# A planner that runs twice and holds each load back until a fixed time ahead of its first use

## The chip, the cores and the metric

The kernel runs on one core of a Trainium2 chip. The metric is the device time of one execution in microseconds (us); lower is better. The kernel before took 425.89 us as the median of three runs (425.65 to 426.75).

## The reference

Two stages follow each other on `B = 4` batches of `N = 12800` rows of width `C = 128`. First an attention through 49 agents: `softmax(agents k^T) v` gives 49 rows per batch (`agent_v`), and `softmax(q agents^T) agent_v` gives one row per query. Then a gated convolution: a causal depth-wise convolution of 5 taps over the rows, a sigmoid of it as the gate, `x @ w_val` as the value, and the product of both through `w_out`:

```
a2k     = sm(agents, k);  agent_v = a2k @ v
x       = sm(q, agents) @ agent_v
gate    = sigmoid(sum_k conv_w[k] * x[t-4+k])
out     = (gate * (x @ w_val)) @ w_out
```

## The kernel before

**Units and chunks.** A batch is cut into 10 units of 1280 rows. Three inputs are loaded unit by unit: `k` and `q` (640 KB each, transposed on the host) and `v` (645 KB). That makes 120 loads. The output is made in 100 chunks of 512 columns, 25 per batch.

**What a unit costs.** TensorE (PE) makes scores of a `k` unit or a `q` unit (L376, 16 matmuls), and for `v` the agent sums (L480). For a `q` unit VectorE, GpSimd (POOL) and ScalarE make the softmax weights `pt`; a DMA transpose (`x<-pt`, L835) turns them into the tile `x1`, and two more DMAs (`x<-x`, L884, "shifts" below) copy shifted rows of `x1` into the tile `x2`. For the first four units PE makes the transposition instead. After the second unit of a pair POOL copies a halo of 4 columns (L819, or a memset, L816) into the next segment of `x1`.

**What a chunk costs.** PE makes the gate (five matmuls on `x1`, L922, and one on `x2`, L926), the value (L949, L953) and the projection of the chunk two before (L992 to L994); ScalarE the tanh (L935), VectorE the product `h` (L962), ScalarE and POOL its two halves `hh` and `hl` (L968, L973), ScalarE the output tile (L1006), and a DMA stores two chunks together (L1021).

**Batches overlap.** While the chunks of one batch run, `k`, `v` and `q` of the next are worked on. In the last batch only its own `q` is left to load. When the last `v` of a batch is through, a short series of small steps (`fold_weights`) makes the weights for its chunks.

**Slots.** The loads share a ring of `NLOAD = 11` tiles (`ld`). Load number n may start when PE has read load n - 11 for the last time. Every load, transpose, shift and store (but one small load at the start) is issued from one queue, that of SyncE (SP), in one order; an issue that waits holds up all that is behind it.

**The planner.** The program does not emit instructions at once. Each piece of work is added to a `Plan` as a step: its engine, an estimated duration, what it reads and writes, and, for a DMA, how long it occupies the wires. `Plan.order()` then plays the steps through, with a clock of its own, one at a time: each engine takes the ready step whose chain of work behind it (`tail`) is longest; a DMA may start when the wires are at most `BACKLOG = 3.0` us behind (L129) and the eighth DMA before it has landed (`LANES = 8`). PE is an exception: each PE step is chained to the one before (L101 to L104), so the order of work on PE is the written order in the string `order` (L1088), whatever the clock says. `order()` returns the steps sorted by their planned start, and the program issues them in that order (L1141). On the chip only this order remains: no engine waits for a planned time.

A load has no input, so in the planner it becomes ready the moment its slot is free (`at = [0.0] * n`, L117, later raised to the end of the slot's last reader).

Of the kernel before, what the change touches and what calls it, by code (L numbers as in the profile page):

```python
# [58 lines left out]
BACKLOG = 3.0  # L59
LANES = 8  # L60
LAND = 1.4

QS = 256.0
WS = 64.0
# [3 lines left out]
class Plan:  # L68
# [11 lines left out]
    def add(self, engine, us, fn, reads=(), writes=(), moved=0.0, key=None, urge=0.0):  # L80
        i = len(self.steps)
        need = set()
        for x in reads:
            need |= self.wrote.get(x, set())
        for x in writes:
            need |= self.wrote.get(x, set()) | self.read.get(x, set())
        for x in reads:
            self.read.setdefault(x, set()).add(i)
        for x in writes:
            self.wrote[x], self.read[x] = {i}, set()  # L90
        self.steps.append((engine, us, fn, need, moved, key))
        self.urge.append(urge)

    def order(self):
        n = len(self.steps)
        after = [[] for _ in range(n)]
        last = None
        for i, (engine, us, fn, need, moved, key) in enumerate(self.steps):
            for j in need:
                after[j].append(i)  # L100
            if engine == "pe":  # L101
                if last is not None and last not in need:
                    after[last].append(i)
                last = i  # L104
        tail = [0.0] * n
        for i in reversed(range(n)):
            engine, us, fn, need, moved, key = self.steps[i]
            cost = us + HOP + (moved + LAND if moved else 0.0)
            if engine == "pe":
                cost = us  # L110
            tail[i] = cost + self.urge[i] + max((tail[j] for j in after[i]), default=0.0)
        engines = ("pe", "act", "dve", "pool", "dma")
        free = dict.fromkeys(engines, 0.0)
        wire = 0.0
        lanes = [0.0] * LANES
        left = [len(s[3]) for s in self.steps]
        at = [0.0] * n  # L117
        queues = {e: [] for e in engines}
        pe = [i for i, s in enumerate(self.steps) if s[0] == "pe"]
        here = 0  # L120
        for i, s in enumerate(self.steps):
            if s[0] != "pe" and not left[i]:
                queues[s[0]].append(i)
        start = [0.0] * n
        kind = None
        done = 0
        while done < n:
            best = None
            free["dma"] = max(free["dma"], wire - BACKLOG, lanes[0])  # L129
            for e in engines:  # L130
                if e == "pe":
                    if here < len(pe) and not left[pe[here]]:
                        pick, when = pe[here], max(free[e], at[pe[here]])
                    else:
                        continue
                elif queues[e]:
                    q = queues[e]
                    soon = min(max(free[e], at[i]) for i in q)
                    open_ = [i for i in q if at[i] <= soon + 0.05]
                    pick = max(open_, key=lambda i: (tail[i], -i))  # L140
                    for i in q:
                        if tail[i] > tail[pick] + 1.0 and at[i] < soon + 0.6 * self.steps[pick][1]:
                            pick = i
                    when = max(free[e], at[pick])
                else:
                    continue
                if best is None or when < best[0]:
                    best = when, e, pick
            when, e, i = best
            engine, us, fn, need, moved, key = self.steps[i]  # L150
            if e == "pe":
                here += 1
                if key != kind:
                    when += 0.12
                kind = key
            else:
                queues[e].remove(i)
            start[i] = when
            free[e] = when + us
            end = when + us + HOP  # L160
            if moved:
                wire = max(wire, when + 0.5) + moved
                end = max(wire, when + us) + LAND
                lanes = lanes[1:] + [end]
            done += 1
            for j in after[i]:
                if i in self.steps[j][3]:
                    left[j] -= 1
                    at[j] = max(at[j], end)
                    if not left[j] and self.steps[j][0] != "pe":  # L170
                        queues[self.steps[j][0]].append(j)
        self.start = start
        return sorted(range(n), key=lambda i: (start[i], i))


@with_exitstack
def tile_agent_attention_gated_conv(
# [22 lines left out]
    plan = Plan()  # L200
    add = plan.add

    def ring(n, shape, dtype, name, pool=const):
        return [pool.tile(shape, dtype, name=f"{name}{i}") for i in range(n)]

    ld = ring(NLOAD, [P, VW], F32, "ld")
# [147 lines left out]
    def load(kind, b, u):  # L354
        i = taken[0] % NLOAD
        taken[0] += 1
        slot_of[kind, b, u] = i
        if kind == "v":
            dst, src = ld[i], vP[b, u].rearrange("p n c -> p (n c)")
        else:  # L360
            dst = ld[i][:, 0:UNIT]
            src = (kT if kind == "k" else qT)[b, :, u * UNIT : (u + 1) * UNIT]
        parts = [(dst, src, [("ld", i), ("ld2", i)])]
        if (kind, b, u) == ("v", 0, NU - 1):
            h = VW // 2
            parts = [(dst[:, 0:h], src[:, 0:h], [("ld", i)]), (dst[:, h:], src[:, h:], [("ld2", i)])]
        for d, f, keys in parts:
            add(
                "dma", 0.4, lambda d=d, f=f: nc.sync.dma_start(out=d, in_=f), (), keys,
                1.57 / len(parts),  # L370
            )

    def score_matmuls(b, src, out):
# [662 lines left out]
    at = (0, 2, 5, 7, 10, 12, 15, 17, 20, 22)  # L1036
# [94 lines left out]
    for w in work:  # L1131
        if w[0] in "qkv":
            while ahead < min(len(loads), NLOAD + done):
                load(*loads[ahead])
                ahead += 1
                if ahead == W_AT:
                    weights()
            done += 1
        run[w[0]](*w[1:])

    for i in plan.order():  # L1141
        plan.steps[i][2]()


# [42 lines left out]
```

## Time and profile before

| | |
|---|---|
| median of three runs | 425.89 us |
| profiled execution, span from first to last instruction | 423.6 us |
| PE busy | 403.9 us (95%) |
| VectorE, ScalarE, POOL busy | 293.3, 301.5, 228.2 us |
| mean granted TensorE clock | 0.985 |
| moved by DMA | 127.62 MB, mean 301 GB/s |

The profile page gives the span of the profiled execution and no other time of it; the median is 2.3 us above the span, which is what lies before the first and after the last instruction. A granted clock of 1.00 is TensorE's upper level of 2.4 GHz, 0.50 is the lower one of 1.2 GHz. "DMA share" is the mean over the 16 DMA engines of the time in which packets were under way; packets of one engine overlap, so it can pass 1. In the tables SPq is SyncE's queue: a start there is the issue of a DMA, and its duration is how long the issue held the queue, not the transfer.

### The profile page before, as it was taken

The numbers are of one execution on the slowest core, as the hardware profiler recorded it, in microseconds if no ns is written. First come the engines' busy times: TensorE is split into PE (matmuls) and PEld (weight loads), VectorE is DVE, ScalarE is ACT, GpSimd is POOL, SyncE is SP. The second block draws the span as 40 slices with busy tenths as digits, with TensorE's granted clock in tenths as the row PEclk, the third lists the DMA queues.
The fourth block names the chain that finished last, engine by engine and source line by source line (L and its number), as shares of the span: only waits on it lengthen the run. The fifth ranks groups of instructions, "written<-read, shape, count | busy, mean of one in ns | idle before, by whom it ended". The sixth has DMA issues, their size and how long they took to land.

```text
span 423.6 us, 10042 instructions
## 1 busy us (share of the span) xinstructions
PE 403.9 (95%) x3907; PEld 197.0 (47%) x3907; DVE 293.3 (69%) x562; ACT 301.5 (71%) x521; POOL 228.2 (54%) x263
## 2 busy tenths in 40 slices
PE   4979999999999999999999899999999989999995
PEld 1358434346555443446555343335555534344443
DVE  3757899867875978667795575767765678676231
ACT  1564568779966777678876486778876567788776
POOL 1002557654657565554566355574366277877553
PEclk9969999999999999999999899999999999999998
DMA  8999999999999999999999999999999977755733
GB/s 320 420 417 411 370 367 353 301 295 310 412 293 283 346 317 362 304 278 356 351 379 324 271 299 370 314 332 302 296 393 322 239 196 161 199 163 176 205 121 124
DMA packets 75129, 127.62 MB, mean 301 GB/s; under 512 B 50466, under 2 KB 50850, under 8 KB 75084
## 3 DMA queue, kind: packets, MB, share of 16 engines
q1 hardware_dynamic: 74940, 126.87, 96.9%
q8 instruction: 30, 0.49, 0.5%
q10 hardware_dynamic: 144, 0.13, 0.2%
q14 instruction: 15, 0.12, 0.1%
HBM read 79.25 MB, written 26.21 MB: 249 GB/s over the span
## 4 chain that ended last, share of the span: by engine, by line
PE 78%; DMA 9%; DVE 8%; ACT 1%; POOL 1%; issue 1%; SPq 0%; POOLq 0%; DVEq 0%; ACTq 0%
PE gate L922 23%; PE sc L376 17%; PE av L480 10%; PE val L949 5%; PE out L992 5%; PE val L953 5%; PE gate L926 5%; PE out L993 4%; DMA ld<-kT 4%; PE out L994 4%; DMA x<-pt 3%; DMA x<-x 2%; DVE h L962 1%; DVE qw L772 1%; DVE qsm L763 1%
## 5 line engine op out<-in xcount | busy, mean ns | idle before, releaser
L973 POOL TENSOR_TENSOR hl<-h,hh 128x512 f16<-128x512 f32 (+1 forms) x101 | 116.9, 1158 | 96.1 <-ACT hh L968 96.0
L922 PE MATMUL gate<-x,stat 128*128 128x512 f16 (+1 forms) x500 | 125.2, 380 | 0.2 <-ACT th L935 0.2
L962 DVE SCALAR_TENSOR_TENSOR h<-th,val 128x512 f32<-128x512 f32 x100 | 67.8, 678 | 66.8 <-PE out L993 26.2
L376 PE MATMUL sc<-ld,ag_sb 128*32 128x320 f32 x1280 | 101.5, 447 | 7.6 <-DMA ld<-kT 7.0
L935 ACT ACTIVATE th<-gate,unscale 128x512 f32<-128x512 f32 x100 | 68.3, 683 | 33.3 <-PE gate L926 31.7
L1006 ACT ACTIVATE ob<-out,oscale 128x512 f32<-128x512 f32 x98 | 67.3, 687 | 21.3 <-PE out L994 20.1
L922 PEld LDWEIGHTS <-stat 128*128 128x128 f16 x505 | 46.3, 97 | 63.7 <-issue 14.8
L968 ACT CAST hh<-h 128x512 f16<-128x512 f32 (+1 forms) x101 | 61.5, 609 | 17.2 <-DVE h L962 16.4
L750 POOL TENSOR_TENSOR qw<-sT,qmx 128x490 f32<-128x490 f32 x40 | 41.4, 1035 | 47.6 <-DVE qmx L745 47.5
L376 PEld LDWEIGHTS sc<-ld,ag_sb 128*32 128x32 f32 x1280 | 36.7, 111 | 59.4 <-issue 25.7
L480 PE MATMUL av<-ld,eT 128*32 128x129 f32 (+1 forms) x1400 | 50.7, 279 | 1.0 <-DVE eT L386 1.0
L480 PEld LDWEIGHTS av<-ld,eT 128*32 128x32 f32 (+1 forms) x1400 | 47.1, 117 | 7.5 <-issue 2.5
L794 POOL TENSOR_TENSOR pt<-qw,pt 128x490 f16<-128x490 f32 x40 | 44.8, 1120 | 3.1 <-ACT pt L779 2.9
L471 ACT ACTIVATE e<-ks,kbias 128x320 f32<-128x320 f32 x80 | 39.3, 554 | 5.4 <-DVE eT L386 3.3
L386 DVE STREAM_TRANSPOSE sT<-sc 128x640 f32<-128x640 f32 x40 | 33.6, 839 | 13.4 <-PE sc L376 12.7
L402 ACT COPY ks<-sc 128x640 f32<-128x640 f32 x40 | 27.7, 691 | 21.2 <-PE sc L376 19.1
L386 DVE STREAM_TRANSPOSE eT<-e 128x640 f32<-128x640 f32 x40 | 33.5, 842 | 9.8 <-ACT e L471 5.2
L926 PE MATMUL gate<-x,stat 95*128 95x512 f16 x100 | 38.3, 383 | 1.5 <-DMA x<-x 1.5
L949 PE MATMUL val<-x,stat 128*128 128x512 f16 x100 | 38.2, 382 | 0.8 <-DVE h L962 0.6
L953 PE MATMUL val<-x,stat 95*128 95x512 f16 x100 | 38.1, 381 | 0.0
L994 PE MATMUL out<-hl,wo 128*128 128x512 f16 x98 | 37.0, 378 | 1.1 <-POOL hl L973 1.1
L992 PE MATMUL out<-hh,wo 128*128 128x512 f16 x98 | 37.3, 381 | 0.1
(130 smaller groups left out, 389.4 us busy)
## 6 DMA issues: line engine op xcount, KB each, us to landing
ld<-kT SPq DMA_DIRECT2D x40, 640.0 KB
ld<-qT SPq DMA_DIRECT2D x40, 640.0 KB
ld<-vP SPq DMA_DIRECT2D x39, 645.0 KB
outT<-ob SPq DMA_DIRECT2D x48, 512.0 KB
x<-x SPq DMA_DIRECT2D x18, 375.0 KB
x<-x SPq DMA_DIRECT2D x18, 100.0 KB
outT<-ob SPq DMA_DIRECT2D x3, 256.0 KB
x<-x SPq DMA_DIRECT2D x4, 187.5 KB
```

Of the source, the lines that this page charges most:

```text
L376: nc.tensor.matmul(out=out[g * BLK : (g + 1) * BLK, j, 0:GT], lhsT=ag_sb[:, b, j * BLK : (j + 1) * BLK], rhs=src[:, g * GT : (g + 1) * GT] ...
L386: nc.vector.transpose(out=out.rearrange("p n (j i) -> p j n i", j=2), in_=in_.rearrange("p j (n i) -> p j n i", i=BLK),)
L480: nc.tensor.matmul(out=av[o + j : o + j + cols, 0 : C + 1], lhsT=et[:, n, j : j + cols], rhs=vt[:, n, :], start=(u == 0 and n < 2), stop=( ...
L922: nc.tensor.matmul(out=pg, lhsT=stat[:, k, :], rhs=x1[:, c : c + w], start=(k == 0), stop=False,)
L926: nc.tensor.matmul(out=pg, lhsT=stat[0 : TAPS * X2R, TAPS + 1, :], rhs=x2[0 : TAPS * X2R, o2 : o2 + w], start=False, stop=True,)
L935: lambda: nc.scalar.activation(out=th, in_=pg, func=AF.Tanh, scale=unscale[:, 0:1]),
L949: nc.tensor.matmul(out=pv, lhsT=stat[:, TAPS, :], rhs=x1s[(b * NCH + n0 // CH) // 5 % NX][:, PAD + o2 : PAD + o2 + w], start=True, stop=False,
L953: nc.tensor.matmul(out=pv, lhsT=stat[0 : TAPS * X2R, TAPS + 2, :], rhs=x2[0 : TAPS * X2R, o2 : o2 + w], start=False, stop=True,)
L962: lambda: nc.vector.scalar_tensor_tensor(out=h, in0=th, scalar=1.0, in1=pv, op0=ALU.add, op1=ALU.mult),
L968: "act", 0.16 + 0.42 * scale, lambda: nc.scalar.copy(out=hh, in_=h),
L973: lambda: nc.gpsimd.tensor_tensor(out=hl, in0=h, in1=hh, op=ALU.subtract),
L1006: lambda: nc.scalar.activation(out=ob[:, o : o + w], in_=po, func=AF.Copy, scale=oscale),
```

## The change

A constant `AHEAD = 14.0` is added; loads get the key `"ld"`; `order()` takes a list of earliest times; and a new method runs `order()` once, reads from it when each load's first reader starts, and runs it again with each load held back to 14 us before that. Nothing else differs. It all happens while the program is built.

```
-    def order(self):
+    def order(self, held=None):
...
-        at = [0.0] * n
+        at = list(held or [0.0] * n)
...
+    def late_loads(self):
+        self.order()
+        held = [0.0] * len(self.steps)
+        for i, s in enumerate(self.steps):
+            for j in s[3]:
+                if self.steps[j][5] == "ld":
+                    t = self.start[i] - AHEAD
+                    held[j] = min(held[j], t) if held[j] else t
+        return self.order(held)
...
             add(
                 "dma", 0.4, lambda d=d, f=f: nc.sync.dma_start(out=d, in_=f), (), keys,
-                1.57 / len(parts),
+                1.57 / len(parts), key="ld",
             )
...
-    for i in plan.order():
+    for i in plan.late_loads():
         plan.steps[i][2]()
```

## Rows read from the trace of the kernel before

**Rows 1.** The page: busy time of the engines, then DMA share in 40 slices.
```profile
PE 403.9 (95%) x3907; PEld 197.0 (47%) x3907; DVE 293.3 (69%) x562; ACT 301.5 (71%) x521; POOL 228.2 (54%) x263
...
DMA  8999999999999999999999999999999977755733
```

**Rows 2.** Stretches of 10 us: busy time of each engine, PE clock, DMA share, GB/s.
```profile
core 0: us, PE busy (x) PEld busy (x) DVE busy (x) ACT busy (x) POOL busy (x), PEclk, DMA share, GB/s
10.00:20.00 10.00, 9.32 (x120) 3.72 (x111) 7.54 (x15) 4.88 (x8) 0.00 (x0) 1.00 1.02 419
...
230.00:240.00 10.00, 8.50 (x107) 4.72 (x100) 5.10 (x14) 3.67 (x7) 4.97 (x7) 0.85 1.14 290
240.00:250.00 10.00, 10.00 (x84) 4.63 (x83) 7.23 (x21) 7.23 (x14) 5.70 (x8) 0.98 1.11 270
...
370.00:380.00 10.00, 10.00 (x50) 4.35 (x52) 7.11 (x13) 8.82 (x16) 8.52 (x10) 1.00 0.64 176
```

**Rows 3.** Waits of PE over the span: us in total, times, longest.
```profile
PE sc L376 <- DMA ld<-kT: 7.0, 4, 6.1
PE gate L926 <- DMA x<-x: 1.5, 1, 1.5
...
PE out L994 <- POOL hl L973: 1.1, 1, 1.1
```

**Rows 4.** Chain that ended last: start us, us, what; near 10, 230 and 335 us.
```profile
7.55 12.53 DMA ld<-kT
...
220.73 7.50 DMA x<-pt
...
228.28 7.34 DMA x<-x
...
331.87 6.86 DMA x<-pt
...
338.78 0.19 POOL x L819
```

**Rows 5.** Timeline of SP's queue: start us, us the queue was held, what.
```profile
10.73 16.74 SPq L369 DMA_DIRECT2D ld<-vP  x11
...
212.77 7.23 SPq L835 DMA_TRANSPOSE x<-pt  x1
...
228.28 1.65 SPq L884 DMA_DIRECT2D x<-x  x2
...
266.97 1.73 SPq L369 DMA_DIRECT2D ld<-vP  x2
...
326.31 2.14 SPq L369 DMA_DIRECT2D ld<-qT  x2
...
361.24 2.94 SPq L835 DMA_TRANSPOSE x<-pt  x2
...
366.46 1.65 SPq L884 DMA_DIRECT2D x<-x  x2
```

**Rows 6.** Chain that ended last, where PE first uses loads.
```profile
26.12 14.19 PE av L480 x200
...
294.50 2.34 PE av L480 x80
...
368.32 1.21 PE sc L376 x16
...
379.83 1.21 PE sc L376 x16
```

**Rows 7.** Timeline of PE: three uses of loads around 220 us.
```profile
219.25 2.41 PE L480 MATMUL av<-ld,eT 128*32 128x129 f32 x80
...
228.85 1.28 PE L376 MATMUL sc<-ld,ag_sb 128*32 128x320 f32 x16
...
241.20 2.09 PE L376 MATMUL sc<-ld,ag_sb 128*32 128x320 f32 x28
```

**Rows 8.** Waits of SP's queue over the span: us in total, times, longest.
```profile
SPq L835 <- POOL hl L973: 48.4, 17, 8.1
```

More of the change, by code (lines that the diff above doesn't have):

```diff
@@ L61 @@
 LAND = 1.4
+AHEAD = 14.0
 QS = 256.0
```

## The prediction

> **What bounds the kernel now.** I read the page first, then the waits of PE, then the chain around the few gaps of PE, then the queue from which the DMAs are issued. PE is busy 403.9 of 423.6 us [rows 1], and the order of its work is written out by hand and not touched, so the change can only move PE's 19.7 idle us and the stretches of low clock. Most of that idle time is out of reach: at the start PE waits 7.0 us for the first keys [rows 3], which no hold can bring sooner, and the rest of the start and the end are short dependent chains. In the body two gaps remain, and both end with a DMA. (A) At 234 us PE waits 1.5 us for a shift, the only wait of that kind [rows 3]. Its chain is a transpose issued at 220.73 that took 7.50 us and a shift issued at 228.28 that took 7.34 us [rows 4]. After the gap the granted clock is 0.85 in that stretch and 0.98 in the next [rows 2]: TensorE falls from 2.4 to 1.2 GHz for a while, which costs 1.5 + 0.2 = 1.7 us more. (B) At 339 us PE waits 1.1 us for `hl` [rows 3], because POOL, in order, sits before the halo copy until a transpose issued at 331.87 lands 6.86 us later, and only then can make `hl` [rows 4].
>
> The second resource is the DMA: its share is above 1 from 10 to 340 us and 0.64 at 370 to 380 [rows 2]. The reader should see the same transposes in both regimes: from the issue of the transpose to the issue of the shift that waits for it is 228.28 - 220.73 = 7.6 us in the crowded part [rows 4, 5], and 366.46 - 361.24 = 5.2 us for a pair of them, so 3.7 us for the second (it starts some 1.5 us later), in the empty part [rows 5]. One transpose even holds SP's queue for 7.23 us at 212.77, where a pair held it for 2.94 us at 361.24 [rows 5].
>
> **What the loads do now.** At the start a load is issued 15.4 us before its use (v: 10.73 against 26.12), later much sooner: 294.50 - 266.97 = 27.5 us, and the last query tile 379.83 - 327.4 = about 52 us [rows 5, 6]. Between, a load can go out as soon as PE frees a slot, 11 loads ahead of its use. So the crowd in the DMA engines is in part work that is not due for 25 us.
>
> **The change, part by part.** It adds and removes no instruction of the chip: the first planner run, the list of holds and the key cost 0 us, since they run at build time. What it moves are the issues of about 85 of the 120 loads (all but the first 35 or so, whose lead is already near 14 us or limited by DMA rate), each later by its present lead less 14: some 10 us in the body, up to 38 us for the last one. A load is moved on SP's queue behind the transposes, shifts and stores that the plan starts in between. On the chip there is no wait for a time: SP issues the load when it gets there.
>
> *Effect on (A).* With a hold the loads issued in 205 to 230 us would be those used 14 us later. PE uses loads at 219.25 (two), then nothing until 228.85 and 229.95, then 241.20 [rows 7]. So loads would go out near 205 to 206.5, three near 215 to 217, and the next at 227. Before the transpose at 212.77, there would be none for 6 us, where now one is ahead whenever a slot came free. Three loads of 0.66 MB at 419 GB/s [rows 2] are 1.57 us each, 4.7 us, over by about 221, and the second transpose at 220.7 and its shift meet an almost empty queue until 227. I take the 7.6 us from transpose to shift down to the quiet 3.7 to 5.2, a gain of 2.4 to 3.9 us, and the shift's 7.34 down by 1 to 2 us. PE needs only 1.5 of that. What is late next is the ordinary chain of a chunk (tanh, product, halves), which PE does not wait for in the chunks around. Bounds: 0 (if the softmax weights of VectorE, not the DMA, set the transpose's time) to -(1.5 + 1.7) = -3.2 us. I take -3.2, because the whole surplus is more than the gap.
>
> *Effect on (B).* The loads before the transpose are now two query tiles at 326.31 that PE uses at 368.32 and 379.83 [rows 5, 6]; they would go at 354.3 and 365.8. I count that an earlier tile, now long there, comes in instead of one of them, so the queue is shorter by one load, 1.57 us, and the transposes ahead stay. Bounds 0 to -1.1 us, taken -0.6.
>
> *What it costs.* Loads that were 15 us early now have a margin of 14 us less the time from issue to landing. The crowded start shows that at its longest: a key tile issued at 7.55 landed 12.53 us later [rows 4]. Held alone, a load still lands 1.5 us before its use. But behind a blocked transpose (7.23 us [rows 5]) it would land 12.53 + 7.23 - 14 = 5.8 us late, and PE would lose that and the 1.7 us of clock that followed gap (A). Bounds 0 to +7.5 us. I take +0.6: near zero, because the long landing time and the long block belong to the crowd that the hold thins out.
>
> Sum: -3.2 - 0.6 + 0.6 = -3.2 us against the profiled span of 423.6. The 2.3 us that lie around the span stay, so from the median: 425.9 - 3.2 = 422.7 us.
>
> A rule speaks against the change. The Trainium skill, "DMA: Bandwidth & Descriptors", section "Rules for kernel authors", tells authors to issue a DMA early, compute, and wait for it late, so that its fixed cost is hidden. This trace agrees only in that no load after the start makes PE wait; by the rule the later issue can only lose, and the time would be that of rival 1 below. What it leaves out, and rows 4 and 5 show, is that an early load delays the urgent transfers queued behind it.
>
> **Rivals.** *1, slower: loads arrive late.* The place is a load that now stands behind a transpose on SP's queue. For it: SP waits long before transposes (17 times for POOL, 48.4 us, at most 8.1 [rows 8]), and with 14 us of lead such a wait and a slow landing do not fit together. Against it: such a wait is there because SP runs ahead of the compute, so what is behind it is early by the plan. It decides from the point where block and landing pass 14 us. One such case at full size is +7.5 us, and with the gains of 3.8 us kept that is 425.9 + 7.5 - 3.8 = 429.6 us; two are 437.
>
> *2, no change: the transposes are hidden anyway.* Both gaps then come from VectorE's late softmax weights. For it: the chain before 220.73 is VectorE work, and the 48.4 us that SP waits before transposes are for compute, not for DMA. Against: after that issue 14.8 us pass in two transfers [rows 4]. Time 425.9, or 424.7 with (B) alone. The hold that changes no order falls here too: if the plan's own leads were below 14 us, the order would stay; the leads of 25 us on the chip [rows 5, 6] speak against that.
>
> *3, faster by more.* Earlier landings also let the planner put other engines' steps in another order. That could take part of the other short waits of PE: about 420 us.
>
> **How the numbers follow.** Forecast (421 to 424.5): 0.49. Rival 1: 0.23. Rival 2: 0.23. Rival 3: 0.05. A measurement of this kernel tells about 0.3%, 1.3 us, from no change, so faster is below 424.6 and slower above 427.2. Faster: 0.49 + 0.05 = 0.54; same: 0.23; slower: 0.23. The range reaches from just below the forecast, 420.6, into rival 1, to 428.6 (a late load of smaller size), which leaves about 0.05 below and 0.13 above. The likeliest case alone has 421.0 to 424.5.
>
> **What would show it.** Right: on SP's queue loads used at 228 to 242 us are issued at 214 to 228; the transpose that held the queue for 7.23 us holds it for less than 3; PE's 1.5 us wait for `x<-x` and the half-clock stretch after it are gone; the DMA share falls below 1 somewhere between 60 and 100 us (the loads' one-time delay) and rises between 340 and 370. Wrong: PE waits for `ld` after 45 us (rival 1), the gap at 234 us still there with a transpose that landed 4 us after its issue (rival 2), or loads issued at the times of before (no new order).

## The result and the profile after

The change made the kernel a little slower: 427.76 us (median; 425.93 to 429.93) against 426.36 us (424.58 to 427.96) for the kernel before in the same comparison, a ratio of 1.0035 with the 95% interval 1.0019 to 1.0051; the medians are 1.4 us apart. I had forecast 422.7 us. The number lies inside the range, which reaches into rival 1, but the direction is wrong. The profiled execution of the changed kernel is one of its quickest, 425.94 us with a span of 423.8 us; two more profiles below show what a slower one of each kernel holds. All lines behind the new planner pass are numbered 13 higher than before.

The page of the changed kernel, busy engines and DMA share [rows 1]:

```profile
PE 401.0 (95%) x3907; PEld 193.8 (46%) x3907; DVE 292.6 (69%) x562; ACT 301.5 (71%) x521; POOL 228.4 (54%) x263
...
DMA  7999997999999999999999999999999999998623
```

Stretches of 10 us, columns as in [rows 2]:

```profile
60.00:70.00 10.00, 10.00 (x90) 4.63 (x92) 9.62 (x20) 8.32 (x14) 6.36 (x8) 1.00 0.74 276
...
190.00:200.00 10.00, 8.16 (x117) 4.32 (x115) 6.41 (x9) 7.07 (x15) 3.71 (x4) 1.00 1.11 331
230.00:240.00 10.00, 9.99 (x129) 5.74 (x128) 7.33 (x17) 6.03 (x10) 5.35 (x6) 1.00 1.16 273
...
300.00:310.00 10.00, 8.63 (x120) 4.75 (x119) 6.04 (x11) 7.12 (x14) 2.46 (x3) 1.00 1.13 274
330.00:340.00 10.00, 10.00 (x129) 5.50 (x128) 6.29 (x13) 5.48 (x10) 4.33 (x6) 1.00 1.08 248
370.00:380.00 10.00, 10.00 (x50) 4.34 (x51) 6.94 (x13) 8.53 (x16) 8.21 (x9) 1.00 1.00 288
```

At 230 us PE is full at full clock, where it had been busy 8.50 at a clock of 0.85 [rows 2]: gap (A) is closed. So is gap (B), at 330. But PE now idles 1.84 us at 190 and 1.37 us at 300. The DMA share dips once, at 60 to 70, and the late stretch at 370 is up from 0.64 to 1.00: the loads did move.

The waits of PE between 60 and 412 us say what the new idle time is for:

```profile
PE av L493 <- DMA ld<-vP: 4.1, 4, 1.6
PE gate L935 <- ACT th L948: 0.2, 1, 0.2
```

The shift's 1.5 us and the 1.1 us for `hl` [rows 3] are gone, and four waits for value tiles stand in their place. They are these on PE's timeline (in brackets the idle time ahead and what ended it):

```profile
193.92 1.31 PE L493 MATMUL av<-ld,eT 128*32 128x129 f32 x40 [1.56 <-DMA ld<-vP]
195.50 1.31 PE L493 MATMUL av<-ld,eT 128*32 128x129 f32 x40 [0.28 <-DMA ld<-vP]
...
295.92 1.31 PE L493 MATMUL av<-ld,eT 128*32 128x129 f32 x40 [0.85 <-DMA ld<-vP]
...
304.49 1.31 PE L493 MATMUL av<-ld,eT 128*32 128x129 f32 x40 [1.37 <-DMA ld<-vP]
```

SP's queue, columns as in [rows 5], shows how these loads came late and how the place of gap (A) looks now:

```profile
185.61 2.04 SPq L382 DMA_DIRECT2D ld<-vP  x2
...
213.96 7.35 SPq L848 DMA_TRANSPOSE x<-pt  x2
221.40 0.54 SPq L382 DMA_DIRECT2D ld<-qT  x1
222.04 0.85 SPq L382 DMA_DIRECT2D ld<-vP  x2
223.49 1.67 SPq L897 DMA_DIRECT2D x<-x  x2
```

The first pair is the one PE stood still for at 193.92: issued 193.92 - 185.61 = 8.3 us before its use, where the planner had put 14. Around (A), two transposes hold the queue for 7.35 us, and the three loads that I had expected at 215 to 217 us go out at 221.4 to 222.9. In the list of SP's waits the line of the transposes grew too, from 48.4 us [rows 8]:

```profile
SPq L848 <- POOL hl L986: 61.9, 17, 8.9
```

These are not waits for compute, though the line names POOL. `hl` is no input of a transpose, and on the timelines of POOL and SP the weights `pt` are ready before each of the 36 transposes starts, in both kernels (at the closest 0.03 us before). The line counts the time in which the issue itself holds the queue. All 36 together hold it for 121.0 us in the kernel before and 140.8 us in the changed one.

What a transpose does to the queue, by its line: the duration of its issue in ns, least, median and most, of 36. The kernel before, and below it the changed one:

```profile
L835 SPq DMA_TRANSPOSE x<-pt x36: 1352/3061/7234, 73.3 to 392.5; - x36
```

```profile
L848 SPq DMA_TRANSPOSE x<-pt x36: 1682/3547/8811, 73.5 to 392.5; - x36
```

The planner counts 1.4 us for each (its cost in the step at L848). On the chip it is 3.5 us in the middle and up to 8.8, and what stands behind it on SP's queue is late by the difference. It is longer where the DMA engines are busier. The two transposes of 361 us, 2.94 us with a DMA share of 0.67 from 360 to 390 us in the kernel before [rows 5], take 6.43 us with the gap between them in the changed one, where that share is 1.03:

```profile
361.19 6.43 SPq L848 DMA_TRANSPOSE x<-pt  x2
```

A table worked out from the traces puts this in one place. The order of PE, VectorE and ScalarE is the same in the kernel before, the changed one and those with leads of 20, 24 and 28 us, so the n-th operation of ScalarE (its table load not counted) can be set against itself. The first column is its start in the kernel before, the others how much later it starts in another execution:

```
n     before   before   changed  changed  lead   lead   lead
      (us)     again             again    20     24     28
98     95.8     +0.4     +0.2     -0.3    -0.6   -0.5   +1.0
178   155.1     +0.6     +0.2     -0.3    -0.6   -0.5   +1.2
218   189.4     +0.6     +0.4     +1.2    -0.6   -0.5   +1.2
258   212.9     +0.6     +2.7     +3.7    -0.6   -0.5   +1.2
278   228.5     +0.7     +2.7     +4.4    -0.6   -0.5   +1.2
298   249.7     +2.0     -0.7     +2.1    -3.9   -3.8   -1.3
358   296.4     +2.0     -0.7     +2.7    -3.9   -3.8   +0.4
378   308.2     +2.0     +2.0     +5.7    -3.9   -3.8   +0.4
418   343.4     +1.4     +0.7     +4.4    -5.2   -5.0   -0.9
438   359.4     +1.4     -0.1     +3.9    -5.9   -5.7   -1.5
518   418.8     +1.4     -0.1     +3.9    -5.5   -5.2   -1.0
```

Read the column of the changed kernel downwards: +2.3 at 190 to 213 us (late loads), -3.4 at 228 to 250 (gap A with its half clock), +2.7 at 296 to 308 (late loads), -2.1 from 308 to 359 (gap B and what stood behind it). The gains are there in full and the loads give them back. The second profile of the changed kernel (next column) gains less at (A), -2.3 us, and loses more: it ends 3.9 us behind.

### The profile page after: what moved, and what is told of

Same layout as the page of the kernel before. It is cut to its first block, busy times and chain, and to the rows that moved or that the text cites. A ratio compares the mean times of both kernels' runs of the same rounds, so it can differ in the third digit from the quotient of the medians.

```text
span 423.8 us, 10043 instructions
## 1 busy us (share of the span) xinstructions
PE 401.0 (95%) x3907; PEld 193.8 (46%) x3907; DVE 292.6 (69%) x562; ACT 301.5 (71%) x521; POOL 228.4 (54%) x263
## 4 chain that ended last, share of the span: by engine, by line
PE 81%; DMA 14%; DVE 2%; ACT 1%; issue 1%; SPq 0%; POOLq 0%; POOL 0%; DVEq 0%
PE gate L935 25%; PE sc L389 18%; DMA ld<-vP 8%; PE av L493 8%; PE val L962 5%; PE out L1005 5%; PE gate L939 5%; PE val L966 5%; PE out L1006 5%; PE out L1007 5%; DMA ld<-kT 4%; DMA x<-x 2%; PE sc L862 0%; DVE qw L785 0%; ACT th L948 0%
## 5 line engine op out<-in xcount | busy, mean ns | idle before, releaser
L493 PE MATMUL av<-ld,eT 128*32 128x129 f32 (+1 forms) x1400 | 49.7, 275 | 5.3 <-DMA ld<-vP 5.2
L493 PEld LDWEIGHTS av<-ld,eT 128*32 128x32 f32 (+1 forms) x1400 | 44.5, 114 | 14.0 <-DVE eT L399 3.6
L399 DVE STREAM_TRANSPOSE sT<-sc 128x640 f32<-128x640 f32 x40 | 33.6, 839 | 13.6 <-PE sc L389 12.7
L424 DVE TENSOR_REDUCE kmx<-ks 128x2 f32<-128x640 f32 x39 | 31.5, 811 | 8.7 <-ACT ks L415 8.7
```

Source lines behind the costliest of these rows:

```text
L399: nc.vector.transpose(out=out.rearrange("p n (j i) -> p j n i", j=2), in_=in_.rearrange("p j (n i) -> p j n i", i=BLK),)
L493: nc.tensor.matmul(out=av[o + j : o + j + cols, 0 : C + 1], lhsT=et[:, n, j : j + cols], rhs=vt[:, n, :], start=(u == 0 and n < 2), stop=( ...
```

## The experiments

Each was timed beside the kernel before on the same chip; intervals are of the ratio to it, 95%. The two without an edit are one profiled execution each. They are told in the order of what they settle.

**The lead, longer and shorter.** If the loads are late because 14 us is too short, a longer lead must keep the gains and lose the waits, and a shorter one must cost more.

```diff
-AHEAD = 14.0
+AHEAD = 20.0
```

> All loads held, but until 20 us ahead of their first use. Theory 'late loads': the hold empties the DMA queue around 220 and 335 us, which removes the two gaps of PE there (about 4 us), but 14 us of the planner are only 6 to 10 us on the chip, because SP is held up by transposes, and loads then land just before or after PE needs them. With 20 us the loads come 12 to 16 us ahead, no wait for loads after 45 us is left, and the gaps stay closed: 2 to 4 us faster than before, 422 to 424.5. Theory 'no gain in it' (the time goes to something else that the hold changes, such as the halo copies' places on POOL or the crowd that moves into the last quarter): within 1 us of the change, about 427.

420.65 us (419.86 to 425.13), ratio 0.989 (0.9845 to 0.9935): faster, by more than I had expected. Its waits of PE between 60 and 412 us are one line, and the three stretches in dispute are full:

```profile
PE gate L935 <- ACT th L948: 0.2, 1, 0.2
```

```profile
190.00:200.00 10.00, 10.00 (x155) 5.80 (x158) 6.89 (x10) 8.82 (x17) 4.86 (x6) 1.00 1.12 343
...
230.00:240.00 10.00, 9.99 (x126) 5.60 (x119) 7.28 (x23) 5.41 (x11) 6.25 (x7) 1.00 1.11 273
...
300.00:310.00 10.00, 10.00 (x92) 4.88 (x91) 6.28 (x11) 8.41 (x16) 5.89 (x6) 1.00 1.04 314
```

Gap (A) stays closed and no load is waited for: hold and late loads are two effects, and 6 us of lead tell them apart.

```diff
-AHEAD = 14.0
+AHEAD = 10.0
```

> All loads held until 10 us ahead. 'Late loads': four us less of a lead that was 6 to 10 us on the chip, with 5 to 9 us from issue to landing: most loads of the body land 1 to 4 us late, in 20 places or more, 8 to 25 us slower than before. 'No gain in it': within 2 us of the change.

431.82 us (429.73 to 435.57), ratio 1.0127 (1.0084 to 1.0169). The direction is that of the late loads; the size is below what I had written, because the lead on the chip fell only from 10.5 to 9.4 us (table below). PE's waits between 60 and 412 us:

```profile
PE av L493 <- DMA ld<-vP: 6.0, 7, 1.9
PE sc L389 <- DMA ld<-kT: 2.3, 5, 1.1
PE sc L389 <- DMA ld<-qT: 1.2, 4, 0.4
```

Together 9.5 us for loads, against 4.1 in the changed kernel.

```diff
-AHEAD = 14.0
+AHEAD = 24.0
```

> All loads held until 24 us ahead. 'Four tight shifts' and 'late loads' together: no load is late, but more loads stand in front of the urgent transfers than at 20 us; between e1 and the kernel before, 420.5 to 424. If margin alone counted, it would be no slower than e1 (420.7).

419.92 us (419.25 to 426.29), ratio 0.9841 (0.9805 to 0.9876), the best of all. Its interval overlaps with that of 20. It has little to spare: in its profile the shifts that PE uses at 94 and 329 us land 0.05 us before their use, and one of its six executions took 426.29 us.

```diff
-AHEAD = 14.0
+AHEAD = 28.0
```

> All loads held until 28 us ahead, close to the lead that the planner gives unheld loads (about 30 us). 'Four tight shifts': with so much lead loads stand in front of the urgent transfers again, 421 to 426, slower than with 24 us. If it is only margin that counts, about 420 as with 24 us.

423.46 us (420.87 to 424.76), ratio 0.9933 (0.99 to 0.9967): still faster than no hold, slower than 24. In PE's waits between 60 and 412 us the shift is back, 1.0 us at 94 us, beside 1.8 us of another chain:

```profile
PE av L445 <- DVE m L438: 1.8, 1, 1.8
PE gate L939 <- DMA x<-x: 1.0, 1, 1.0
```

So the lead has an optimum between two costs. What the leads became on the chip, from the timelines of SP and PE, for the 90 loads used after 60 us (us). A load has landed with the last count of its semaphore, for which PE waits; its last packet, by which the expectations count (22 loads under 2 us with 14), ends about 0.5 us earlier in the median:

```
kernel                 planned  issue to use  landing to use  loads landing
                       (median)   (median)    least/median    under 2 ahead
no hold (before)         29.7       24.8        4.7 / 16.3          0
28                       27.5       20.2        4.2 / 12.3          0
24                       23.6       17.1        4.2 /  9.4          0
20                       19.8       15.1        2.9 /  6.9          0
14 (the change)          14.0       10.5        0.1 /  2.7         34
10                        8.9        9.4        0.0 /  1.5         50
14, transpose 4.0 us     13.3       13.6        0.0 /  4.8          4
24, transpose 4.0 us     18.2       17.7        2.3 /  9.7          0
```

SP's timeline says what stands in front of the 34 loads with 14 us: they are issued 5.4 us later than 14 us before their use, in the mean, and of these 5.4 us the issues of transposes hold the queue for 2.5, those of other loads for 1.0, of shifts for 0.6 and of stores for 0.5; the rest are waits, most of them before shifts and loads.

**One kind of load free.** If the value tiles are the late ones, freeing them must take their waits away.

```diff
-                1.57 / len(parts), key="ld",
+                1.57 / len(parts), key="ld" if kind != "v" else None,
```

> All k and q loads held until 14 us ahead, v loads not held. 'Late loads': the waits of PE for v (5.2 us in the profile of the change, 4 of them after 45 us) are gone, the closed gaps stay closed: 423 to 425.5, 2 to 4 us faster than the change; some waits for k and q may stay. 'No gain in it': about 427, as the change.

424.94 us (423.33 to 427.62), ratio 0.9979 (0.995 to 1.0007), 2.8 us below the changed kernel's median. No value tile is waited for after 60 us; what is left are query tiles, still held at 14:

```profile
PE sc L389 <- DMA ld<-qT: 3.4, 4, 1.6
```

The wait goes with the load that is held, and comes at the next kind that is.

**The planner told what a transpose costs.** This leaves 14 us and mends the planner's clock instead.

```diff
             add(
-                "dma", 1.4,
+                "dma", 4.0,
                 lambda: nc.sync.dma_start_transpose(
```

> The change (14 us), with one more edit: the planner is told that a transpose holds the DMA queue for 4.0 us instead of 1.4 (the chip holds it 3.5 us in the median of the change). 'SP is held up by transposes': the planner's leads are then met on the chip, with a median of 12 to 14 us instead of 10.5; few loads land less than 2 us ahead of their use (22 of 90 in the change), and it is 2 to 6 us faster than the change, 421.5 to 425.5. If the lead shrinks for another reason, it stays at 10 to 11 us and the time at 426 to 429. The planner also puts some VectorE, ScalarE and POOL steps elsewhere, which alone may move it by 1 us or so.

425.77 us (423.4 to 428.78), ratio 0.9985 (0.9955 to 1.0014). The lead came out as planned (13.6 us on the chip, 13.3 by the plan), 4 loads instead of 34 land within 2 us of their use, and no load is waited for after 60 us. That is what the late-load theory asks for. But the time is slightly above what I had expected. The planner, with another cost, also moved steps of other engines (at 90 of the 521 places in ScalarE's order stands another operation), and PE now waits for ScalarE; that the moved steps are the cause was not tried alone:

```profile
PE gate L935 <- ACT th L948: 2.9, 3, 1.9
PE sc L389 <- ACT ks L415: 1.7, 1, 1.7
```

```diff
-AHEAD = 14.0
+AHEAD = 24.0
...
-                "dma", 1.4,
+                "dma", 4.0,
```

> The same told cost of 4.0 us, held until 24 us ahead: the candidate for the best version. With no late loads on either side, 418.5 to 421.5; not slower than 24 us alone (419.9) unless the other engines' moved steps cost something.

423.83 us (421.37 to 426.05), ratio 0.9931 (0.99 to 0.9962): a miss, it does not add up with the lead of 24. The plan itself reaches a lead of only 18.2 us in the median there; on the chip it is 17.7, about that of 24 alone (17.1), so the lead is not what sets the two apart. Why it is slower was not settled.

**Where the gain comes from.** The prediction put it into one place, gap (A). So I held only the six loads around it:

```diff
-AHEAD = 14.0
+AHEAD = 14.0; HELD = (("q", 2, 4), ("k", 3, 0), ("k", 3, 1), ("k", 3, 2), ("k", 3, 3), ("q", 2, 5))
...
-                1.57 / len(parts), key="ld",
+                1.57 / len(parts), key="ld" if (kind, b, u) in HELD else None,
```

> One part alone: only the six loads issued between 208 and 226 us in the kernel before (two query and four key units) are held until 14 us ahead; all others go as before. 'Late loads': the gap at 234 us and the half-clock stretch behind it are gone and nothing else is late: 2 to 3.5 us faster than before, 422.5 to 424.5. 'No gain in it': no change, 426 +- 1.

426.78 us (422.45 to 428.47), ratio 0.9995 (0.9963 to 1.0027): no change, a miss. The gap at 234 us is gone from its profile (span 426.2), yet others stand elsewhere on PE's timeline:

```profile
95.90 0.38 PE L939 MATMUL gate<-x,stat 95*128 95x512 f16 x1 [1.96 <-DMA x<-x]
...
333.54 0.39 PE L939 MATMUL gate<-x,stat 95*128 95x512 f16 x1 [1.76 <-DMA x<-x]
...
345.62 1.24 PE L935 MATMUL gate<-x,stat 128*128 128x512 f16 x5 [2.00 <-ACT th L948]
```

Two of them are the same kind of wait, for a shift, at other chunks. In the first profile of the kernel before, the shifts used at 94, 136 and 333 us had landed only 0.3, 1.2 and 4.0 us ahead of PE; with (A) these are the four tight places that I looked at (two more, at 63 and 406 us, had 2.4 and 4.1 us), and which of them stalls differs from one execution to the next. The kernel before, profiled once more with no edit, tests this:

> The kernel before, one more profile. 'Four tight shifts': its idle time in the body is not bound to one place: the waits of PE for shifts and for hl sum to 2 to 5 us again, but at another of the four places (94, 136, 235, 333 us) than the 1.5 us at 234. Otherwise: the same gap at 234 us and none at the others.

427.01 us, span 425.0. Gap (A) is there again, larger, and one at 94 us that the first profile did not have. A line of PE's timeline, and PE's waits after 60 us:

```profile
237.71 0.39 PE L926 MATMUL gate<-x,stat 95*128 95x512 f16 x1 [2.89 <-DMA x<-x]
```

```profile
PE gate L926 <- DMA x<-x: 3.8, 2, 2.9
PE val L949 <- DVE h L962: 0.6, 1, 0.6
PE out L994 <- POOL hl L973: 0.5, 1, 0.5
```

Then only the loads in front of the four tight shifts were held, 34 of the 90, at 20 us:

```diff
-AHEAD = 14.0
+AHEAD = 20.0; HELD = "k2.0 k2.1 k2.2 ... v3.8 v3.9".split()
...
-                1.57 / len(parts), key="ld",
+                1.57 / len(parts), key="ld" if f"{kind}{b}.{u}" in HELD else None,
```

> Only 34 of the 90 loads used after 60 us are held, until 20 us ahead: those that the kernel before issues in front of the four shifts that land less than 4.5 us before PE needs them (PE at 94, 136, 235 and 333 us). Theory 'four tight shifts': the gain of the 20 us hold comes from these four places, because loads no longer stand in front of the urgent transposes and shifts there; holding one group alone (e3) left the other three to stall. Expected: most of the gain of e1, 421 to 423.5, no wait of PE for a shift after 60 us. Theory 'a thinner crowd everywhere': the gain needs all loads held, so about a third of it, 424.5 +- 1.

423.64 us (421.02 to 428.86), ratio 0.9919 (0.9892 to 0.9946): about three quarters of what holding all at 20 gives (0.81% of 1.1%, the intervals overlap). No shift is waited for after 60 us; PE's longest wait there is of another kind, which the profiles of 20 and 24 don't have:

```profile
PE av L445 <- DVE m L438: 2.3, 1, 2.3
```

**Another queue for the loads.** Loads that do not stand behind transposes should not come late.

```diff
-                "dma", 0.4, lambda d=d, f=f: nc.sync.dma_start(out=d, in_=f), (), keys,
+                "dma", 0.4, lambda d=d, f=f: nc.scalar.dma_start(out=d, in_=f), (), keys,
```

> The change as it is (14 us), but loads are issued from ScalarE's queue instead of SP's, at the same places of the plan. 'Late loads': their lead shrinks from 14 us to a median of 10.5 because they stand behind transposes that hold SP's queue; behind ScalarE's work they keep 13 us or more, and PE's waits for loads after 45 us (4.1 us in the profile of the change) are gone or below 1 us. ScalarE pays about 0.35 us for each of 120 issues on top of its 301 us, so the whole time can go either way: 421 to 428. If instead the landing itself is what is slow, the leads stay near 14 but the waits for loads stay as well.

534.86 us (526.47 to 547.26), ratio 1.2359 (1.2293 to 1.2425): far off. The issue of a load waits on ScalarE's own queue for another DMA, and the operations behind it wait with it. Two lines of ScalarE's timeline, its queue and the operation behind, and PE's longest wait:

```profile
238.92 0.33 ACTq L382 DMA_DIRECT2D ld<-vP  x1
239.30 0.61 ACT L771 ACTIVATE qw<-qw 128x490 f32<-128x490 f32 x1 [8.62 <-DMA x<-x]
```

```profile
PE gate L935 <- ACT th L948: 50.0, 11, 11.4
```

ScalarE stands idle for 8.62 us until a shift has landed and the load is out. The run therefore says nothing on late loads, and that transposes on the same queue are the largest part of what delays them rests on SP's timeline and on the planner told 4.0 us.

**The changed kernel again**, with no edit, for a second profile:

> The change, one more profile, since the first was of one of its quickest executions. 'Late loads': waits for loads after 45 us of 4 us or more again, at v loads and at some k or q; no wait of PE for a shift at 234 us. If the first profile's waits were chance, they are gone or below 2 us.

430.42 us, span 427.7. PE's waits between 60 and 412 us hold 7.5 us for loads, keys and queries among them, and none for a shift:

```profile
PE av L493 <- DMA ld<-vP: 4.3, 3, 1.8
PE sc L389 <- DMA ld<-kT: 2.9, 4, 0.9
PE sc L389 <- DMA ld<-qT: 0.3, 1, 0.3
```

## Why the prediction was wrong, point by point

**(A), -3.2 us: right.** The gap and the half-clock stretch go: -3.4 us between 228 and 250 us in the changed kernel's column (-2.3 in its second profile), -3.3 with leads of 20 and 24. The reason given was only half right. The transposes do not hold the queue for less than 3 us each there (4.5 and 2.8 us for the two at 213.96), and the median of all from issue to landing hardly moved, 7.5 to 7.4 us. From the second of them, issued at 218.51, to the shift's issue are 223.49 - 218.51 = 5.0 us, down from 7.6 as forecast. The shift itself was to be 1 to 2 us quicker and is slower: its larger part takes 8.4 us from issue to landing (7.3 before [rows 4]), but issued 4.8 us sooner it lands 3.7 us sooner, at 231.9 against 235.6, which is more than the 1.5 us that PE had stood still for. What changed is the order on the queue: no load stands between the two transposes any more, where one issued at 220.10 had, for a use at 252.6. In the changed kernel the late loads before (A), which put PE's use of this shift off, add to the margin; with 20 and 24 us they don't, and the shift lands 0.8 and 2.3 us ahead.

**(B), -0.6 us: right in kind, too small.** The columns of 14, 20 and 24 fall by 1.2 to 1.3 us between 308 and 343 us, and by 0.7 to 0.8 more behind it (the 0.6 us for `h` in the profile before). And the gaps of one execution are not all that the kernel before has: its second profile carries 4.8 us of them.

**The cost of late loads, +0.6 us of a range of 0 to +7.5: this is the step that failed.** Measured by PE's waits it is 4.1 us in a quick execution and 7.5 in a slower one. I took the low end "because the long landing time and the long block belong to the crowd that the hold thins out". The hold thins it little: the DMA share is still above 1 in the stretches shown from 190 to 340 us. Of the loads used after 60 us the median from issue to landing fell by 1.3 us (8.4 to 7.1), that of the shifts' larger part by 0.9 (6.7 to 5.8), but the longest load still takes 12.3 us (12.6 before), and the transposes hold the queue longer. Against rival 1 I had set that what stands behind a waiting transpose "is early by the plan". With a hold nothing is early by the plan: every load is planned at 14 us, and the plan's 14 are 10.5 on the chip (least 5.9), mostly because its transposes are 1.4 us long. From those, 7.1 us in the median and 12.3 at the longest go into the landing. Under it lies a misreading, in rivals 1 and 2 alike: the 48.4 us [rows 8] are not SP waiting for compute but part of the 121.0 us for which the issues of transposes hold the queue, and they hold it just as long in front of a load that is due soon.

**Rival 1 was the right one, with another shape.** I had priced it as one big case of 7.5 us. It is many small ones, 0.3 to 1.8 us each, spread over value, key and query tiles. With the gains kept as 20 keeps them (-5.5 us at the end of its column), the loads must cost about 7 us in the median execution for +1.4 us, which agrees with the second profile.

**The rule weighed against the change holds on one side.** The leads of 10 and 14 us lose to no hold (ratios 1.0127 and 1.0035), but 20, 24 and 28 beat it (0.989, 0.9841, 0.9933). The Trainium skill, "DMA: Bandwidth & Descriptors", section "Rules for kernel authors", would have a DMA issued early and waited for late. By that rule every hold loses; the first two runs agree with it, and the other three differ. What it leaves out is the shifts: with no hold PE waits 1.5 and 3.8 us for them in the two profiles, with 20 and 24 us not at all.

**Open.** The halo copies of POOL also stand in other places (with 14, 20 and 24 us another operation stands at 19 to 21 of the 263 places in its order); their share was not tried alone. The wait for `th` at 345 us with six loads held, and for `m` at 287 us with 34 held and at 28 us, have no cause shown.

## What to carry to other kernels

A just-in-time hold is worth its while where urgent small transfers share a queue with bulk loads, but the lead must be counted in the chip's time: issue to landing under load, plus what the transposes ahead hold the queue, plus a margin, not what a planner's costs say. Before a line of waits is read as waiting for compute, look at when the input was ready. Sweep the lead before judging the idea: here the same few lines are worth +1.3% at 10 us, +0.35% at 14, -1.1% at 20, -1.6% at 24 and -0.7% at 28. And when stalls move between executions, take two profiles of the kernel before: a gap seen in one is only one of several tight places.

## What the runs showed of the hardware

A DMA transpose's issue held SP's queue for 1.4 to 8.8 us in the two kernels, 3.1 and 3.5 us in the median, although its input was ready, and what stood behind it waited. Five transposes between 361 and 386 us held it for 1.35 to 1.47 us each with a DMA share of 0.67 (before), and for 2.3 to 3.8 us with one of 1.03 (changed); the share alone does not set it, since one of the changed kernel took 1.7 us at 115 us, where the share was 1.09. And an issue that has to wait stops the engine whose queue it is on: loads issued from ScalarE cost 24%. SP computes nothing; its 36 transposes held it for 140.8 us in the changed kernel, and PE lost 4.1 us by late loads.
